# Key projections in three PSUM banks, and GpSimd's weight sums held back by a one-column copy

## The chip, the cores and the metric

The kernel runs on one core of one Trainium2 chip. The metric is the device time of one execution in microseconds (us), in most places as the median of several executions. One profiled execution of each kernel gives a trace with the start and duration of every instruction.

## The reference

A polynomial sketch attention, whose output is the input of four expert layers, mixed by gates:

```python
def phi(x):                                  # x: (4, 4, 1088, 32), S1 and S2: (8, 32)
    a = np.einsum('rd,bhsd->bhsr', S1, x)
    b = np.einsum('rd,bhsd->bhsr', S2, x)
    return np.einsum('bhsi,bhsj->bhsij', a, b).reshape(*x.shape[:-1], 64)
q_p, k_p = phi(q), phi(k)
kv = np.einsum('bhsf,bhsd->bhfd', k_p, v)
num = np.einsum('bhsf,bhfd->bhsd', q_p, kv)
den = np.einsum('bhsf,bhf->bhs', q_p, np.sum(k_p, axis=2))[..., None] + 1e-06
# x = num / den, as (4352, 128)
for e in range(4):                           # F = 1024
    h = np.maximum(x @ w1[e], 0.0)
    out += p[:, e:e + 1] * (h @ w2[e])       # p: gates, scaled to sum 1
```

## The kernel before

The tokens are worked off in chunks. A chunk's expert layers are 16 steps, each a product `h = x w1` into one of three PSUM banks "h", a rectification into `hid` (ScalarE and VectorE) and a product `o = hid w2`. The attention that prepares later tokens is cut into small pieces, laid between the steps. All matmuls go through one helper, which lets two halves of the array (64 columns of weights each) take turns. They run side by side. The trace records each call as two matmuls:

```python
def on_side(out, weights, moving, **flags):
    s = turn[0]
    turn[0] = 1 - s
    nc.tensor.matmul(out(s), weights(s), moving(s), **flags)
```

The keys of batches 1 to 3 pass through this generator. Each `yield` is a place where other work may come between:

```python
def keys(b):
    for r in range(3):
        key_turn(b, r)                          # VectorE transposes
        yield
    for gi in range(3):
        key_project(b, gi, psum(ps_f, "f"))     # 32, 32 and 8 recorded matmuls, then a ScalarE copy to fs
        yield
    ...                                         # products, and key sums in bank "f" again
```

The pool of "f" has one bank, those of "den" and "num" too. A projection into "f" can only start when ScalarE has copied the one before out of it.

The second product of the experts uses sums and differences of blocks of w2. GpSimd forms them, 16 instructions in all; the main loop puts one behind each step from step 13 on:

```python
def weight_sums(e):
    ...
        nc.gpsimd.tensor_tensor(out=out, in0=in0, in1=in1, op=op)    # two inputs in SBUF
        yield
...
        first(i, work)              # h, the rectification, and pieces of attention
        if i > NQ - 4:              # NQ = 16
            next(to_sum, None)
        if i == 2:
            gate_quotients()
        elif i == 5:
            store_gates()           # one VectorE transpose, then transfers
            ...                     # loads of two gates and of the next batch
```

GpSimd has little else to do there, so it runs ahead of the steps: the sums come as soon as it is free, beside VectorE's products for the second unit of 480 queries:

```python
def query_product(qp, p, x, n, qa, qb):
    nc.vector.tensor_tensor(out=qp[p][64*x : 64*x+64, 0:n],
        in0=qa[64*p : 64*p+64, 0:n], in1=qb[64*p : 64*p+64, 0:n], op=ALU.mult)    # two inputs in SBUF
```

These four products are what the matmuls into "den" and "num" wait for.

## Time and profile before

| | before |
|---|---|
| median of the first three executions | 498.6 us (498.53 to 499.03) |
| span of the profiled execution | 496.7 us |
| busy: TensorE matmuls / weight loads / VectorE / ScalarE / GpSimd | 99 / 74 / 65 / 49 / 46% |

A matmul's record includes time in which the next one already runs (a projection's matmul is recorded with 0.22 us, and 32 of them take 1.12 us on the two halves), so a busy TensorE isn't a full one; its waits tell more. In the timeline, a line has the start, the duration, the engine, the source line, the operation, its output and inputs with their shape, and how many instructions it merges; in brackets the idle time ahead of it and what ended that. PE is TensorE's matmuls, PEld its weight loads, DVE VectorE, ACT ScalarE, POOL GpSimd. L188 is the helper's line, so one goes by the names of the tiles: `f<-sk,kT` is a key projection, `fs<-f` its copy, `qp<-qa,qb` the products for the queries, `w2s` the weight sums.

### The profile page before, as it was taken

The page shows a single profiled execution, that of the slowest core. Times are in us where ns is not written, and L with a number is a line of the kernel's source. Part 1 is how long each engine was busy: PE and PEld are TensorE (multiplying, and loading weights), DVE is VectorE, ACT ScalarE, POOL GpSimd, SP SyncE. Part 2 cuts the span into 40 slices and gives each one's busy share as a digit, 9 for nine tenths or more (in the row PEclk, how much of TensorE's full clock was granted, in tenths as well). Part 3 has the DMA queues.
Part 4 walks back from the last instruction along what each step waited for, and adds up shares of the span by engine and source line. Part 5 has one row for each costly group of instructions (what it writes and reads, how often), then busy time and mean ns, then how long its engine had stood idle before and what let it go on. Part 6 is the DMA issues. An engine that isn't in the chain of part 4 may idle for free.

```text
span 496.7 us, 11022 instructions
## 1 busy us (share of the span) xinstructions
PE 489.3 (99%) x4435; PEld 367.8 (74%) x4435; DVE 324.8 (65%) x751; ACT 244.0 (49%) x487; POOL 228.2 (46%) x259
## 2 busy tenths in 40 slices
PE   8999999999999999999999999999999999999996
PEld 6776577777777657777776777777777777778996
DVE  6859756777677485767656747468666656765642
ACT  3334455445444544535455455445455445566651
POOL 6600544444455353434555344334555345655570
PEclk9999999999999999999999999999999999999999
DMA  7881030021002230021002100021001100110000
GB/s 219 270 294 54 0 92 1 2 86 21 0 2 86 66 91 0 1 86 22 1 2 86 21 1 1 2 86 22 2 1 53 23 1 0 45 23 2 15 3 17
DMA packets 29618, 22.36 MB, mean 45 GB/s; under 512 B 19968, under 2 KB 26752, under 8 KB 29184
## 3 DMA queue, kind: packets, MB, share of 16 engines
q1 hardware_dynamic: 29552, 21.66, 15.1%
q8 instruction: 35, 0.57, 0.5%
q14 instruction: 15, 0.12, 0.1%
q10 hardware_dynamic: 16, 0.00, 0.0%
HBM read 19.35 MB, written 2.31 MB: 44 GB/s over the span
## 4 chain that ended last, share of the span: by engine, by line
PE 98%; DVE 1%; issue 0%; ACT 0%; DVEq 0%
PE h L188 49%; PE o L188 40%; PE f L188 5%; PE den L188 2%; PE num L188 1%; PE h L176 1%; DVE qp L412 1%; ACT fs L344 0%; DVE qa L471 0%; DVE end L648 0%; DVE end L644 0%; DVE xT L446 0%; DVE kvz L374 0%; DVE warm L135 0%; DVE s_hl L212 0%
## 5 line engine op out<-in xcount | busy, mean ns | idle before, releaser
L584 DVE SCALAR_TENSOR_TENSOR hid<-h,hid 128x256 f32<-128x256 f32 (+6 forms) x432 | 203.7, 472 | 148.0 <-ACT hid L609 139.7
L188 PE MATMUL h<-xT,w_sb 128*64 128x512 f32 (+4 forms) x1408 | 299.7, 496 | 0.4 <-DVE xT L446 0.4
L609 ACT ACTIVATE hid<-h 128x512 f32<-128x512 f32 (+3 forms) x288 | 158.2, 550 | 200.5 <-PE h L188 169.8
L188 PE MATMUL o<-hid,w2s 128*64 128x256 f32 (+3 forms) x1152 | 220.8, 355 | 0.0
L188 PEld LDWEIGHTS h<-xT,w_sb 128*64 128x64 f32 x1408 | 148.2, 137 | 52.2 <-issue 12.9
L188 PE MATMUL o<-hid,w_sb 128*64 128x256 f32 (+3 forms) x864 | 184.5, 355 | 0.0
L188 PEld LDWEIGHTS o<-hid,w2s 128*64 128x64 f32 x1152 | 133.1, 137 | 29.0 <-issue 2.7
L724 POOL TENSOR_TENSOR ev<-yz,sh 64x256 f32<-64x256 f32 (+3 forms) x72 | 48.5, 674 | 160.5 <-ACT sh L727 154.7
L188 PEld LDWEIGHTS o<-hid,w_sb 128*64 128x64 f32 x864 | 102.4, 137 | 21.4 <-issue 6.6
L712 POOL TENSOR_TENSOR yz<-ev 128x512 f32<-128x512 f32 (+3 forms) x36 | 42.2, 1172 | 80.8 <-ACT ev L715 80.5
L724 POOL TENSOR_TENSOR ct<-ev 128x512 f32<-128x512 f32 (+3 forms) x36 | 42.6, 1182 | 2.8
L724 POOL TENSOR_TENSOR ct<-ct,gate 128x512 f32<-128x512 f32 (+3 forms) x27 | 32.0, 1186 | 2.1
L724 POOL TENSOR_TENSOR total<-total,ct 128x512 f32<-128x512 f32 (+3 forms) x27 | 31.9, 1180 | 2.1
L412 DVE TENSOR_TENSOR qp<-qa,qb 64x352 f32<-64x352 f32 (+2 forms) x44 | 30.2, 687 | 1.1
L714 ACT COPY ev<-o 128x512 f32<-128x512 f32 (+3 forms) x36 | 19.4, 538 | 10.1 <-PE o L188 9.6
L188 PE MATMUL o<-w_sb,hid 128*64 128x128 f32 x256 | 24.2, 273 | 0.0
L188 PEld LDWEIGHTS o<-w_sb,hid 128*64 128x64 f32 x256 | 20.1, 137 | 1.5 <-issue 1.2
L715 ACT COPY ev<-o 128x512 f32<-128x512 f32 (+3 forms) x36 | 19.4, 538 | 2.8 <-PE o L188 0.5
L601 ACT ACTIVATE hid<-h 128x256 f32<-128x256 f32 x24 | 9.2, 383 | 22.8 <-PE h L188 22.3
L351 DVE TENSOR_TENSOR kp<-fs 128x256 f32<-128x256 f32 (+1 forms) x24 | 16.7, 704 | 0.0
L727 ACT COPY sh<-yz 64x256 f32<-64x256 f32 (+3 forms) x36 | 13.7, 379 | 1.6 <-POOL yz L712 0.8
L728 ACT COPY sh<-yz 64x256 f32<-64x256 f32 (+3 forms) x36 | 13.7, 380 | 0.9
(95 smaller groups left out, 244.3 us busy)
## 6 DMA issues: line engine op xcount, KB each, us to landing
w_sb<-in_moe_w_dram SPq DMA_DIRECT2D x8, 512.0 KB, 7.4
gate<-gates SPq DMA_DIRECT2D x3, 1024.0 KB, 4.6
kn<-in_k_dram SPq DMA_DIRECT2D x4, 544.0 KB, 4.0
vn<-in_v_dram SPq DMA_DIRECT2D x16, 128.0 KB, 4.0
gate<-gates SPq DMA_DIRECT2D x2, 960.0 KB
qn<-in_q_dram SPq DMA_DIRECT2D x3, 544.0 KB, 3.8
gate<-gates SPq DMA_DIRECT2D x1, 896.0 KB
out_dram<-ob SPq DMA_DIRECT2D x12, 64.0 KB, 2.0
```

Source lines behind the costliest of these rows:

```text
L188: nc.tensor.matmul(out(s), weights(s), moving(s), **flags)
L351: eng.tensor_tensor(out=_ap(kps[b], 0, P, 256 * t0 + P * p + 64 * x, [[256, n], [32, 2], [R, 4], [1, R]]), in0=_ap(src, 0, P, off + 4 * x, ...
L412: nc.vector.tensor_tensor(out=qp[p][64 * x : 64 * x + 64, 0:n], in0=qa[64 * p : 64 * p + 64, 0:n], in1=qb[64 * p : 64 * p + 64, 0:n], op=A ...
L584: nc.vector.scalar_tensor_tensor(out=out, in0=src, scalar=0.0, in1=in1, op0=ALU.max, op1=ALU.subtract)
L601: nc.scalar.activation(hd[:, 0 : 2 * n], hp[:, 0 : 2 * n], ACTF.Relu)
L609: nc.scalar.activation(hd[:, n * j : n * j + n], hp[:, 0:n], ACTF.Relu)
L712: add = lambda out, in0, in1, op=ALU.add: nc.gpsimd.tensor_tensor(out=out, in0=in0, in1=in1, op=op)
L714: nc.scalar.copy(_ap(ev, 0, P, 0, [[2 * w, 2], [1, w]]), _ap(a0, 0, P, 0, two))
L715: nc.scalar.copy(_ap(ev, 0, P, w, [[2 * w, 2], [1, w]]), _ap(a1, 0, P, 0, two))
L724: add = lambda out, in0, in1, op=ALU.add: nc.gpsimd.tensor_tensor(out=out, in0=in0, in1=in1, op=op)
L727: nc.scalar.copy(sh[HP:P, 0:w], yz[0:HP, 0, 0:w])
L728: nc.scalar.copy(sh[0:HP, 0:w], yz[HP:P, 1, 0:w])
```

## The change

Both parts are meant to take away stops of TensorE: neighbouring projections no longer share a bank, and the sums no longer run beside the products. The second is done with a copy of one column that GpSimd can't make before the second unit's x is there. The sums come behind it in GpSimd's program, and the trace below shows them behind it in time too (27.07 and 27.21 us). The diff in full:

```diff
-        for gi in range(3):
-            key_project(b, gi, psum(ps_f, "f"))
+        for gi, (pool, tag) in enumerate(((ps_f, "f"), (ps_n, "den"), (ps_n, "num"))):
+            key_project(b, gi, psum(pool, tag))
             yield
@@
+    behind = cpool.tile([P, 1], F32, name="behind")
     start()
@@
             first(i, work)
             if i > NQ - 4:
+                if i == NQ - 3:
+
+                    nc.gpsimd.tensor_copy(behind[:, :], xT[:, CHUNKS[0] + CHUNKS[1] - 1 : CHUNKS[0] + CHUNKS[1]])
                 next(to_sum, None)
```

## The prediction

> **What bounds the kernel now.** I read the page from its chain of waits, since an average over the span cannot say where 499 us go. The chain that ended last:
>
> ```profile
> PE 98%; DVE 1%; issue 0%; ACT 0%; DVEq 0%
> PE h L188 49%; PE o L188 40%; PE f L188 5%; PE den L188 2%; PE num L188 1%; PE h L176 1%; DVE qp L412 1%; ACT fs L344 0%; DVE qa L471 0%; DVE end L648 0%; DVE end L644 0%; DVE xT L446 0%; DVE kvz L374 0%; DVE warm L135 0%; DVE s_hl L212 0%
> ```
>
> TensorE carries 98% of the end. 89% is the two products of the expert layers (h and o), which the change doesn't touch. The change can win only time in which TensorE stands still. The next view is the waits by engine, longest first, cut to TensorE's matmuls (PE) and weight loads (PEld); columns are total us, times, longest:
>
> ```profile
> PEld f L188 <- ACT fs L344: 1.7, 3, 0.6
> ...
> PEld den L188 <- DVE qp L412: 1.4, 3, 0.7
> PE f L188 <- ACT fs L344: 0.9, 2, 0.5
> ...
> PE den L188 <- DVE qp L412: 0.4, 1, 0.4
> ```
>
> A PE wait is mostly the same stop as the PEld wait before it, so they must not be added. The two parts of the change aim at exactly these: "f <- fs" is a key projection waiting for ScalarE to copy the one before out of the only bank "f"; "den <- qp" is the attention waiting for VectorE's feature products. Together about 3 us of 499, or 0.6%. That is the ceiling for both parts, and it decides the verdict already. The rest of this text is about how much of it comes back.
>
> The place of the second, in the timeline from 15 to 24 us (start, duration, engine, operation):
>
> ```profile
> 19.75 1.09 DVE L412 TENSOR_TENSOR qp<-qa,qb 64x480 f32<-64x480 f32 x1
> 20.85 1.09 DVE L412 TENSOR_TENSOR qp<-qa,qb 64x480 f32<-64x480 f32 x1
> ...
> 20.29 1.14 POOL L494 TENSOR_TENSOR w2s<-w_sb 128x256 f32<-128x256 f32 x1
> 21.39 1.15 POOL L494 TENSOR_TENSOR w2s<-w_sb,w2s 128x256 f32<-128x256 f32 x1
> ...
> 46.43 0.65 DVE L412 TENSOR_TENSOR qp<-qa,qb 64x480 f32<-64x480 f32 x1
> ...
> 23.79 1.30 PE L188 MATMUL den<-qp,kvz 128*64 128x480 f32 x3 [0.42 <-DVE qp L412]
> 24.48 0.13 PEld L188 LDWEIGHTS den<-qp,kvz 128*64 128x64 f32 x1 [0.50 <-DVE qp L412]
> ```
>
> The same VectorE product takes 1.09 us while GpSimd forms weight sums and 0.65 us (the line at 46.43) when it doesn't; the sums go from 0.73 to 1.14. And the first projections of the second batch:
>
> ```profile
> 61.63 1.01 PEld L188 LDWEIGHTS f<-sk,kT 128*64 128x64 f32 x32 [0.60 <-ACT fs L344]
> 61.64 1.15 PE L188 MATMUL f<-sk,kT 128*64 128x64 f32 x32 [0.46 <-ACT fs L344]
> ```
>
> TensorE stands still while ScalarE's 0.37 us copy empties the bank.
>
> **What the Trainium skill says.** "Perfetto Trace Analysis", Matmuls under Optimizing Tensor Performance, advises that independent matmul groups rotate through different PSUM banks so that one group's evacuation overlaps the next group's matmuls; the 0.46 us gap above is what not rotating costs here. The same page, Identifying the Most-Contended Engine, warns that matmul busy share is no measure of nearness to the limit; agreed, PE shows 99% and the weight loads 74%, so I read stops and not shares. "SBUF — State Buffer", Who interferes with whom, says that a VectorE instruction with two SBUF inputs contends with a GpSimd instruction that reads SBUF, and that one with at most one SBUF input doesn't. The trace agrees in kind: qp (two SBUF inputs) is stretched, while the addition into qf, which reads one input from PSUM, takes 0.66 us with the sums running (17.18) and 0.66 without (38.58). The page says the loser blocks for the whole instruction; 1.09 is less than 0.65 + 0.73, so the measured stretch is what I use.
>
> **Part 1, three banks.** It adds and removes no instruction. The three projections of a batch now go into f, den and num. Batches 1 to 3 use this path (batch 0 has its own), so there are six places where a projection follows another:
> - Batch 1, second projection: the first one's 32 matmuls start at 60.05 and go at about 0.031 us each (1.0 us for 32), so the next could start at 61.07; it starts at 61.64. Won: 0.57. Its third is a step later, without a wait: 0.
> - Batch 2, second: PEld waits 0.48, but four matmuls of h at 0.21 each (from 166.09, one before it) keep the array busy until about 166.73 and the projection starts at 166.84. Won: 0.1.
> - Batch 2, third: could start at 166.84 + 1.0 = 167.85, starts at 168.50. Won: 0.63.
> - Batch 3: expert steps lie between all three, and no wait for fs is shown: 0.
>
> Sum 1.3 us, on the path. Are den and num free? They were last read by VectorE's transpose dT and by the product that writes xT, both ahead of the key transposes on VectorE itself, which the projections need anyway. No new wait there. The attention that next writes den comes many us after the copies.
>
> **Part 2, the held sums.** It adds one GpSimd copy of one column, 0.1 to 0.2 us by the small GpSimd operations at 10 to 12 us (0.12 to 0.30). It depends on the write of xT that ends at 28.19, so the nine sums that ran from 15.92 to 23.22 start after it. On VectorE, three of the four qp products were stretched: 1.09, 1.09 and 0.98 against 0.65, together 0.44 + 0.44 + 0.33 = 1.2 us. The chain from there to den has no other waits, so the last product ends at 24.43 - 1.2 = 23.2 and the one before it at about 22.5. TensorE's loads are free at 23.79 - 0.66 = 23.13. So the first wait (0.66) goes, and of the second (0.50 more) about 0.1 stays. The two 64-column halves of the array run side by side, and both must be through before ScalarE can rectify. A check on that: ScalarE's rectifications come every 0.87 us, but 3.81 us apart (23.47 to 27.28) across den and num. Den and num are four matmul passes of 0.4 us on each half, so 1.6 + 0.87 = 2.47 was due, and 1.3 us were lost. I count **1.15 us** won, all on the path.
>
> What it gives back: the first matmul with a summed weight starts at about 37.1. xT would be ready near 27.0, and sums at 0.73 us each finish expert 0's four by 27.2 + 2.9 = 30.1 and all nine by 33.8, against 36 for that matmul. GpSimd had nothing else from 23.22 to 48.79, so nothing queues behind them. VectorE's work from 27 to 34 (a transpose, hid and end, each with at most one SBUF input or one from PSUM) isn't of the stretched kind.
>
> **Sum.** 1.3 + 1.15 = 2.45 us off 498.6, or 496.15. I take 496.2, because a wait elsewhere may eat a tenth.
>
> **Rivals.**
> 1. Taking away a stop only moves it: the projections finish sooner, and the next h matmul waits for VectorE to free one of the three h banks. For it: PEld h waits for hid 1.3 us in 7 pieces of at most 0.3. Against it: after the projections VectorE had ended its hid at 61.98, before h comes at 63.6. If true for part 1, some 1 us is not won: 497.2.
> 2. The held sums run late, and GpSimd or the first w2s matmul becomes the wait. The slack is some 6 us for expert 0. If xT's hold pushed the sums behind the first collection at 48.8, several us would be lost: 500 or more. The nine sums take 6.6 us in a hole of over 20, so I give this little.
> 3. The waits were never on the path (the other half of the array would have hidden them): 498.6 stays. The 3.81 against 2.47 us speaks against it for part 2, the 98% chain for both.
> 4. More than counted is won, because earlier work upstream also closes small "issue" gaps: 495.3 at best.
>
> **Range and chances.** All rivals but the second lie within 495.3 and 498.6; the three runs before lie within 0.5 us. I set 495.2 to 497.3. Faster by over 2% would need 10 us, three times all of these waits: 0.01. Slower by over 2% needs the second rival at its worst: 0.01. Within 2%: 0.98.
>
> **What would show it.** In the changed kernel: no wait of f, den or num for ScalarE's fs; all four 480-column qp products at 0.65 us; GpSimd's first sum after xT, near 27 us; the wait of den for qp down from 1.4 to 0.3 us or less; the first summed matmul near 36; ratio of busy times unchanged. Wrong would be: sums at 1.1 us again beside other VectorE work, a wait of o for the sums, or a wait of h for hid that grew by as much as was won.

## The result, and the profile after

The changed kernel took 496.11 us (median of 6, 495.90 to 496.64), beside 498.81 us (median of 6, 498.48 to 499.29) for the one before. The ratio is 0.9947 with an interval of 0.9934 to 0.9960, so some 2.6 us are gone.

In the waits view of the changed kernel (total us, times, longest), no wait of f, den or num for fs is left. Of the three waits of den for qp, the short one stays, which belongs to a later unit. GpSimd's new wait is the first line here:

```profile
POOL behind L788 <- DVE xT L446: 11.1, 1, 11.1
...
PEld den L188 <- DVE qp L412: 0.2, 1, 0.2
```

The timeline of the changed kernel from 19 to 37 us, engine by engine:

```profile
19.79 1.31 DVE L412 TENSOR_TENSOR qp<-qa,qb 64x480 f32<-64x480 f32 x2
...
21.90 1.34 DVE L412 TENSOR_TENSOR qp<-qa,qb 64x480 f32<-64x480 f32 x2
...
23.22 1.10 PE L188 MATMUL den<-qp,kvz 128*64 128x480 f32 x4
...
27.07 0.18 POOL L788 COPY behind<-xT 128x1 f32<-128x1 f32 x1 [11.07 <-DVE xT L446]
27.21 0.72 POOL L494 TENSOR_TENSOR w2s<-w_sb 128x256 f32<-128x256 f32 x1
...
32.93 0.73 POOL L494 TENSOR_TENSOR w2s<-w_sb 128x256 f32<-128x256 f32 x1
...
36.27 0.37 PE L188 MATMUL o<-hid,w2s 128*64 128x240 f32 x1
```

The two pairs of products now take 1.31 and 1.34 us where they took 2.19 and 1.67 (19.75 to 21.94, and 22.76 to 24.43). Den starts at 23.22 and not 23.79, and its four matmuls take 1.10 us, where the first three alone took 1.30. The nine sums run from 27.21 to 33.66 and are ready well ahead of the first matmul that uses one, at 36.27.

What the stop cost shows in ScalarE's rectifications, which need both halves of the array. First the pair around den and num in the kernel before, then in the changed one:

```profile
23.47 0.38 ACT L601 ACTIVATE hid<-h 128x256 f32<-128x256 f32 x1 [0.49 <-PE h L188]
27.28 0.38 ACT L601 ACTIVATE hid<-h 128x256 f32<-128x256 f32 x1 [3.42 <-PE h L188]
```

```profile
23.52 0.38 ACT L601 ACTIVATE hid<-h 128x256 f32<-128x256 f32 x1 [0.49 <-PE h L188]
26.09 0.38 ACT L601 ACTIVATE hid<-h 128x256 f32<-128x256 f32 x1 [2.20 <-PE h L188]
```

The pair is 3.81 us apart before and 2.57 after: 1.24 us less.

The second batch's first projections in the changed kernel follow each other without a gap; where the two halves change banks at different moments, the lines alternate:

```profile
58.87 1.19 PE L188 MATMUL f<-sk,kT 128*64 128x64 f32 x29
...
59.90 0.22 PE L188 MATMUL den<-sk,kT 128*64 128x64 f32 x1
59.90 0.22 PE L188 MATMUL f<-sk,kT 128*64 128x64 f32 x1
...
60.28 0.37 ACT L344 COPY fs<-f 128x256 f32<-128x256 f32 x1 [0.36 <-PE f L188]
...
61.21 0.37 ACT L344 COPY fs<-den 128x256 f32<-128x256 f32 x1 [0.56 <-PE den L188]
```

ScalarE empties f while TensorE is already in den.

**A ruler for small differences.** Executions differ by up to 0.7 us in their first 10 us: the first 72 projection matmuls took 2.32 us in the traces of the two kernels above, and 2.41 to 2.80 in eight of the experiments' eleven traces. So I also measure from a fixed event: from the last rectification ahead of den (23.47 before, 23.52 after) to the start of VectorE's last scaling of an output (492.81 before, 490.18 after). That is 469.34 us before and 466.66 after: **2.68 us less**. The copies that collect finished products (36 in each kernel) show where. Counted from the same rectification, they come 0.98 us earlier from the first one (46.4 us), 1.90 earlier by 89 us, 2.68 earlier by 171 us, and then stay there to the end. So everything came from den and from the projections of batches 1 and 2, and nothing was given back later.

### The profile page after: what moved, and what is told of

Same layout as the page of the kernel before. It is cut to its first block, busy times and chain, and to the rows that moved or that the text cites. A ratio compares the mean times of both kernels' runs of the same rounds, so it can differ in the third digit from the quotient of the medians.

```text
span 494.1 us, 11020 instructions
## 1 busy us (share of the span) xinstructions
PE 487.7 (99%) x4435; PEld 373.7 (76%) x4435; DVE 323.2 (65%) x751; ACT 244.2 (49%) x487; POOL 227.2 (46%) x260
## 4 chain that ended last, share of the span: by engine, by line
PE 98%; DVE 1%; DMA 0%; POOL 0%; issue 0%; DVEq 0%
PE h L188 50%; PE o L188 40%; PE f L188 4%; PE den L188 2%; PE num L188 2%; DMA s_raw<-in_S_dram 0%; PE h L176 0%; POOL sr L241 0%; POOL sp L236 0%; DVE end L648 0%; DVE s_e L200 0%; DVE kvz L374 0%; DVE s_f L200 0%; DVE s_T L228 0%; DVE s_hl L227 0%
## 5 line engine op out<-in xcount | busy, mean ns | idle before, releaser
L188 PEld LDWEIGHTS h<-xT,w_sb 128*64 128x64 f32 x1408 | 151.2, 137 | 48.8 <-PE h L176 0.9
L188 PEld LDWEIGHTS o<-hid,w2s 128*64 128x64 f32 x1152 | 131.7, 137 | 29.1
L412 DVE TENSOR_TENSOR qp<-qa,qb 64x352 f32<-64x352 f32 (+2 forms) x44 | 29.1, 661 | 1.1
L188 PE MATMUL o<-w_sb,hid 128*64 128x128 f32 x256 | 22.4, 273 | 0.0
L188 PEld LDWEIGHTS o<-w_sb,hid 128*64 128x64 f32 x256 | 19.0, 137 | 1.5 <-issue 0.2
```

Of the source, the lines that this page charges most:

```text
L412: nc.vector.tensor_tensor(out=qp[p][64 * x : 64 * x + 64, 0:n], in0=qa[64 * p : 64 * p + 64, 0:n], in1=qb[64 * p : 64 * p + 64, 0:n], op=A ...
```

## The experiments

My theory: the two parts act separately, part 1 by having neighbours in different banks (1.46 us), part 2 by keeping GpSimd's SBUF reads away from VectorE's products (1.2 us). Eleven kernels, all correct, five rounds each; they ran in sets on three chips, each set beside the kernel before, whose median was 498.7 to 498.9 us every time. In the table, "ruler" is the length just defined, less that of the kernel before.

| kernel | median us | ratio to before | ruler us |
|---|---|---|---|
| changed kernel | 496.11 | 0.9947 | -2.68 |
| banks_only | 497.38 | 0.9972 | -1.48 |
| hold_only | 498.00 | 0.9984 | -0.98 |
| two_banks | 496.02 | 0.9946 | -2.68 |
| one_bank_num | 498.83 | 1.0001 | 0.00 |
| sums_twice | 497.22 | 0.9970 | -1.54 |
| fills_early | 496.08 | 0.9944 | -2.68 |
| sums_late | 499.70 | 1.0018 | -0.05 |
| hold_gates_later | 497.73 | 0.9981 | -0.98 |
| both_gates_later | 496.48 | 0.9951 | -2.68 |
| hold_free_chain | 497.67 | 0.9977 | -0.98 |
| both_free_chain | 496.51 | 0.9952 | -2.68 |

### banks_only: the first part alone

```diff
# against the changed kernel
-                if i == NQ - 3:
-
-                    nc.gpsimd.tensor_copy(behind[:, :], xT[...])
```

> The three banks without the held sums. My theory: the two parts add up, and in the trace with both, the start of ScalarE's collection copies moved by 0.67 us in the first of the batches with this path and by 0.79 in the second, nothing in the third: 1.46 us in all. So 498.8 - 1.45 = 497.35 us, ratio 0.9971; qp products still at 1.09 us, no wait of f, den or num for fs. Rival (the two parts hide behind each other, so that one alone gives nothing or all): 498.8 or 496.1.

It took 497.38 us, ratio 0.9972 (0.9960 to 0.9985). On the ruler it gains 0.70 us in batch 1 and 0.78 in batch 2. In batch 1 the second projection now starts 0.93 us after the first, where the kernel before needed 1.59 (60.05 to 61.64):

```profile
60.77 1.12 PE L188 MATMUL f<-sk,kT 128*64 128x64 f32 x32
61.70 1.12 PE L188 MATMUL den<-sk,kT 128*64 128x64 f32 x32
```

The wait of den for qp is the old one, no wait for fs is left:

```profile
PEld den L188 <- DVE qp L412: 1.4, 3, 0.7
...
PE den L188 <- DVE qp L412: 0.4, 1, 0.4
```

### hold_only: the second part alone

```diff
# against the changed kernel
-        for gi, (pool, tag) in enumerate(((ps_f, "f"), (ps_n, "den"), (ps_n, "num"))):
-            key_project(b, gi, psum(pool, tag))
+        for gi in range(3):
+            key_project(b, gi, psum(ps_f, "f"))
```

> The held sums with all three projections in bank f. Theory: 1.2 us off, since the rectification after den came 1.19 us earlier with both parts: 497.6 us, ratio 0.9976; waits of f for fs remain at about 1.7 us of weight loads, three times. Rival (parts hide behind each other): 498.8 or 496.1.

It took 498.00 us, ratio 0.9984 (0.9972 to 0.9997): 0.85 us of the median, less than expected and more than nothing. The products are at 0.65 us, and the waits for fs are as they were. Its rectifications around den are 2.58 us apart, so den gave its 1.2 us here too; but the collection copies come only 0.98 us earlier. Where the difference goes shows in the second batch. Its first projection starts at 59.16, which is 35.36 us after the rectification ahead of den, against 36.58 in the kernel before: 1.22 us earlier. The second starts at 60.99, only 0.98 us earlier by the same count:

```profile
59.16 1.37 PE L188 MATMUL f<-sk,kT 128*64 128x64 f32 x32
...
60.99 1.15 PE L188 MATMUL f<-sk,kT 128*64 128x64 f32 x32 [0.46 <-ACT fs L344]
```

The 32 matmuls of the first take 1.37 us from the first start to the last end, where the kernel before needed 1.12: one half of the array is some 0.25 us ahead of the other. The copy must wait for the half behind, and the next projection for the copy, so this lead is not used. With other banks, the half ahead goes on. The parts alone add up to 1.48 + 0.98 = 2.46 us, and together they are 2.68.

### two_banks: are three needed?

```diff
# against the changed kernel
-enumerate(((ps_f, "f"), (ps_n, "den"), (ps_n, "num"))):
+enumerate(((ps_f, "f"), (ps_n, "den"), (ps_f, "f"))):
```

> Held sums, and projections in f, den, f. Theory: what counts is that neighbours are in different banks; by the time of the third projection the copy of the first has ended over 1 us ago. So the same as the changed kernel: 496.1 us, ratio to before 0.9947, and no wait for fs. Rival (three banks are needed): the third projection of the third batch waits as before, some 0.6 us more: 496.7.

It took 496.02 us, ratio 0.9946, the same 2.68 us on the ruler and no wait for fs. Two banks in turn do all of it.

### one_bank_num: is it bank f?

```diff
# against the kernel before
-            key_project(b, gi, psum(ps_f, "f"))
+            key_project(b, gi, psum(ps_n, "num"))
```

> The kernel before, but all three projections in the bank num instead of f: one bank still, another one. Theory: the wait comes from one bank having to be emptied, not from what else uses f (the queries and the key sums), so nothing is won: 498.8 us, ratio 1.000, and the same waits, now of num for fs, 1.7 us of weight loads. Rival (leaving f is what helps, because queries or key sums queue there): part of the 1.45 us is won, 497.4 to 498.

It took 498.83 us, ratio 1.0001 (0.9988 to 1.0013), 0.00 on the ruler. The waits have changed their name and nothing else:

```profile
PEld num L188 <- ACT fs L344: 1.7, 3, 0.6
...
PE num L188 <- ACT fs L344: 0.9, 2, 0.5
```

### sums_twice: GpSimd's reads back beside the products

```diff
# against the changed kernel
                 if i == NQ - 3:
+                    twice = chain.from_iterable(weight_sums(e) for e in range(3))
+                    for _ in range(9):
+                        next(twice)
                     nc.gpsimd.tensor_copy(behind[:, :], xT[...])
```

> The changed kernel, with the nine sums formed twice: once early and unheld, as the kernel before had them, and once behind xT. Theory: the gain of the held sums was the absence of GpSimd's reads beside VectorE's qp products. So those products go back to 1.09, 1.09 and 0.98 us, and den waits again for 1.2 us: 496.1 + 1.2 = 497.3 us. Rival (it was the place of the sums in GpSimd's order, or what they delay later): the held copies still come at 27 us, so 496.1.

It took 497.22 us, ratio 0.9970, so 1.1 us more than the changed kernel; on the ruler 1.14. The held sums are still there, at 28.53 us. The products are slow again:

```profile
19.87 2.21 DVE L412 TENSOR_TENSOR qp<-qa,qb 64x480 f32<-64x480 f32 x2
22.88 1.68 DVE L412 TENSOR_TENSOR qp<-qa,qb 64x480 f32<-64x480 f32 x2
```

So it is what runs beside the products that counts, not what else the sums' new place brings.

### fills_early: GpSimd busy there, but only writing

```diff
# against the changed kernel
                 if i == NQ - 3:
+                    for _ in range(7):
+                        nc.gpsimd.memset(w2s[:, 3, :, :, :], 0.0)      # later overwritten by the sums
                     nc.gpsimd.tensor_copy(behind[:, :], xT[...])
```

> The changed kernel, with seven fills of 128x1024 by GpSimd where the sums used to run, about 1 us each: GpSimd as busy as before, but it reads nothing. Theory: two SBUF inputs of VectorE contend with GpSimd's reads only, so the qp products stay at 0.65 us and the time at 496.1. Rival (any GpSimd work in SBUF slows them): products near 1.1 us, 497.3.

It took 496.08 us, ratio 0.9944, the same 2.68 on the ruler. GpSimd was busy during all but the last 0.28 us of the products, and they didn't get longer:

```profile
16.54 7.02 POOL L788 MEMSET w2s<- 128x1024 f32 x7
...
20.39 1.31 DVE L412 TENSOR_TENSOR qp<-qa,qb 64x480 f32<-64x480 f32 x2
...
22.50 1.34 DVE L412 TENSOR_TENSOR qp<-qa,qb 64x480 f32<-64x480 f32 x2
```

Together with sums_twice this shows that GpSimd's sums, which read SBUF, cost, and fills that only write there don't.

### sums_late: how long could the sums be held?

```diff
# against the changed kernel
                     nc.gpsimd.tensor_copy(behind[:, :], xT[...])
+                    for _ in range(9):
+                        nc.gpsimd.memset(w2s[:, 3, :, :, :], 0.0)
```

> The changed kernel, with nine fills of 128x1024, about 1 us each, between the held copy and the first sum. Tests the slack that I counted: the first four sums would end at 27.2 + 9 + 2.9 = 39.1 us where the first matmul with a summed weight came near 35.9. Theory: TensorE waits 3.2 us there for the sums, all of it on the path: 499.3 us, and the wait is shown as o for w2s. Rival (the slack is longer, or other work fills the wait): 496.1.

The profiled execution took 499.11 us; on the ruler it is 2.63 us longer than the changed kernel. TensorE waits for the third sum, which ends at 38.86 us, and with its weight loads for the fourth, which ends at 39.55:

```profile
36.62 0.57 PE L188 MATMUL o<-hid,w_sb 128*64 128x240 f32 x2
38.92 1.31 PE L188 MATMUL o<-hid,w2s 128*64 128x240 f32 x6 [1.74 <-POOL w2s L494]
...
39.60 0.20 PEld L188 LDWEIGHTS o<-hid,w2s 128*64 128x64 f32 x4 [0.49 <-POOL w2s L494]
```

So the slack was counted about right (2.63 us for 3.2 expected), and held much longer, the sums would eat the gain. The six executions scatter more than any others here: three at 498.54 to 499.19 us with a mean granted clock of 0.999 to 1.000, three at 500.22 to 500.74 with 0.995. Whether the longer stop of TensorE brings on the lower clock is not settled by six executions.

### hold_gates_later and both_gates_later

The 0.22 us that the parts gain together, and one candidate for a better version, led to two pairs of kernels. In the first, the storing of the gates, whose 0.33 us transpose lies between the shuffle and the products on VectorE, comes five steps later:

```diff
# against hold_only, and against the changed kernel
-            elif i == 5:
+            elif i == 10:
                 store_gates()
                 ...            # three loads (two gates, the next batch) move with it
```

> Held sums, one bank, and the storing of the gates (on VectorE one transpose of 0.33 us between the shuffle and the first qp product, then transfers) five steps later, after the last qp product. What it is for: alone, the held sums gave 0.85 us by the clock and 0.98 in the trace, where 1.2 was expected. Theory: the 0.2 us wait that den keeps for its second qp tile leaves one half of the array about 0.25 us ahead of the other, and the next wait for fs, which stops both, takes that lead away. With the transpose gone from the chain the second tile is ready before TensorE asks, neither half leads, and the whole 1.2 us is kept: 497.6 us, collection copies 1.2 us earlier than before when counted from the rectification ahead of den. Rival (the 0.25 us is lost elsewhere): 498.0 and 0.98 us as with the held sums alone.

> The changed kernel with the same move of the gates' storing; the candidate that may beat both. Theory: the last 0.2 us wait of den for qp goes, so 0.2 us less at most: 495.9 us, and no wait of den for qp in the trace. Rival (the lead of one half is worked off by the other anyway): 496.1. A later gate could also delay the first gate products on GpSimd near 55 us, but these have 20 us to arrive.

They took 497.73 us (0.9981) and 496.48 us (0.9951), and stand on the ruler at -0.98 and -2.68, each to 0.01 us where the same kernel stood without the move. The edit failed to do what it was for. In hold_gates_later, VectorE waited for TensorE instead, ahead of a scaling that comes next, so the products ended as late as ever, and den's four matmuls still took 1.10 us. (The 0.2 us wait that the expectation speaks of was misread: in the waits view it is the later unit's. What den itself has left is at most the 0.1 us by which 1.10 exceeds the 1.00 of the next pair.)

```profile
19.54 0.35 DVE L644 TENSOR_SCALAR end<-o,ends 128x128 f32<-128x128 f32 x1 [0.32 <-PE o L188]
```

### hold_free_chain and both_free_chain

So in the second pair that scaling went behind the products too:

```diff
# on top of the edit above; in the last product of the first chunk's first expert
-                    nc.vector.tensor_scalar(out=total[m][:, :], in0=acc[m][:, 0:DM], scalar1=p_e, ...)
+                    later.append(scale)        # the same instruction, given out ahead of the next expert's
```

> Moving the gates' transpose alone freed nothing: VectorE then waited for TensorE in front of the scaling that comes next, and the qp products ended when they had. Here both, the transpose and that scaling (0.33 and 0.35 us), come after the last qp product; held sums, one bank. Theory: the products end some 0.65 us earlier, den waits for nothing, no half of the array leads, and the held sums keep their 1.2 us: collection copies 1.2 us earlier than before counted from the rectification ahead of den, 497.6 us. Rival (the lead of a half isn't what takes 0.25 us): 0.98 us as with the held sums alone, 497.9.

> The same with the three banks; the last candidate. Theory: at most the 0.2 us of den's remaining wait for qp goes: 495.9 us and no such wait in the trace. Rival: 496.1, the wait was hidden by the other half.

They took 497.67 us (0.9977) and 496.51 us (0.9952). This time the edit worked: the last product ends 0.81 us ahead of the rectification in hold_free_chain (23.21 and 24.02), and 0.27 in hold_only (23.53 and 23.80). Den's matmuls start in step, 1.00 us for the four instead of 1.10, and the rectifications around den are 2.48 us apart instead of 2.58. Yet the ruler shows -0.98 and -2.68 again. So the 0.1 us won at den is gone by the end, and my theory that den's remaining wait gives one half its lead falls: with den in step, hold_free_chain's first projection is again spread out:

```profile
57.67 0.57 PE L188 MATMUL h<-xT,w_sb 128*64 128x480 f32 x1
...
58.04 1.77 PE L188 MATMUL h<-xT,w_sb 128*64 128x480 f32 x7
59.28 1.46 PE L188 MATMUL f<-sk,kT 128*64 128x64 f32 x32
```

The source and the traces point to where the lead comes from, though no run tested it. In these chunks a step's second product is seven calls that take turns, so one half gets four and the other three, and the next step does the reverse. A call lasts some 0.4 us here (two matmuls, 0.2 us apart), so the halves are in step and 0.4 us apart by turns. In hold_free_chain they leave den and num in step (0.04 us), and the step ahead of the first projection finds them 0.37 us apart (57.67 and 58.04 above). In the kernel before, the stop at den leaves one half 0.43 us ahead (its next h begins at 26.15, the other's at 26.58), which swaps the turns: there the step ahead of the projection finds them in step (eight matmuls of h in 1.80 us from 58.44), and the projection takes 1.12 us. That the lead is thrown away at the wait for fs, and kept with other banks, is what the traces show. Neither candidate beats the changed kernel. Their medians are 0.4 us above it, but with the same length on the ruler and a start that is 0.6 us later in their profiled executions. Traces of one_bank_num and fills_early, whose edits act only after that start, have it too (rectification at 24.19 and 24.11); whether the two edits here have a part in it isn't settled.

## Why the prediction was right

- **The total.** Predicted 496.2 us, measured 496.11; predicted 2.45 us off, measured 2.7 by the medians and 2.68 on the ruler.
- **The bound and the ceiling.** TensorE stayed 98% of the chain of waits. Only its stops could be won, and their sum (3 us) bounded the gain.
- **Part 1, 1.3 us: right, a little small.** Alone it gave 1.47 us by the medians and 1.48 on the ruler. Batch 1: 0.57 predicted, 0.70 measured. The prediction let a projection last 1.02 us before the next; it lasts 0.93 (60.77 to 61.70 in banks_only), which is 0.09 of the difference. The rest is the second projection, 0.98 us to the next matmul after the wait and 0.94 without it. Batch 2: two terms were off and largely cancelled. The second projection gained nothing where 0.1 was predicted (1.79 us behind the first in both kernels, 165.05 to 166.84 and 165.06 to 166.85), so that its wait was hidden by h altogether; the third gained 0.78, not 0.63. Batch 3: 0 and 0.
- **No new wait in den or num: right.** No run with these banks shows one; two_banks shows that num wasn't needed.
- **Part 2, 1.15 us: right on top of part 1, too large alone.** On top of the three banks it gave 1.20 on the ruler (2.68 - 1.48). Alone it gave 0.98 there and 0.85 by the medians. The text treated the parts as independent, and the term that it lacked is the 0.22 us which a wait in bank f takes back from it. That its 1.15 us hit the sum so well needed the other part beside it.
- **The mechanism of part 2: right, and shown** by sums_twice (reads: slow, 1.14 us lost) and fills_early (writes: nothing lost).
- **What it gives back: right.** All sums ended at 33.66 (predicted 33.8), and the first matmul that uses one came at 36.27. (In the kernel before that matmul starts at 37.45; the 37.1 of the prediction is the one ahead of it, with a plain weight.) Rival 2 came about only when sums_late held the sums 9 us longer, and then cost 2.63 us.
- **The other rivals.** A stop that only moves (rival 1) would have left h waiting for hid; the waits view of the changed kernel shows no such wait. That the waits were off the path (rival 3) is refuted by the 1.48 us of part 1. Of rival 4, 0.2 us more than counted came true, but not for its reason: the terms above were too small by 0.18 (part 1) and 0.05 us (part 2). Most of the "issue" gaps closed in hold_only (weight loads of h: 13.5 to 1.9 us), which won less than counted.
- **A sign that I misnamed.** "Ratio of busy times unchanged" was loose: the weight loads' busy time rose from 367.8 to 373.7 us for the same 4435 loads. Their single times add up to the same in both traces (607.6 and 607.5 us), so they overlap each other less; no run tested why.

## What to carry to other kernels

When one engine is on the path for 98% of the span, add up its waits by cause before judging a change: the sum is the ceiling, and here it said "under 1%" at once. Let neighbouring groups of matmuls alternate between two banks if an engine must empty one between them; more than two won nothing here. Before moving work to an idle GpSimd, look at what VectorE does then: reads from SBUF beside a VectorE operation with two SBUF inputs cost (here 1.09 us and not 0.65 for a product), and a copy that depends on the right tile is a cheap way (0.18 us) to hold such work back, as long as its user has slack.

## What the Trainium skill lacked or had wrong

- "SBUF — State Buffer", Summary: rules for kernel authors: it says that of VectorE and GpSimd the second to come blocks fully until the first has finished. Here VectorE's products rose from 0.65 to 1.09 us and GpSimd's sums from 0.73 to 1.14 while both ran, starting in turn every 0.54 to 0.56 us (19.75, 20.29, 20.85, 21.39). That fits blocking by turns, if about half of each record is waiting: the product that starts at 22.76, behind a sum that ends at 23.22, ends at 23.74. No run shows the waiting itself. What the page lacks is the cost: one pair took 1.1 us, and 0.65 + 0.73 would be 1.38, so whole records aren't what excludes the other. What the page says under Who interferes with whom of a GpSimd instruction that only writes is right: beside fills, the products stayed at 0.64 to 0.66.
- "TensorE: Matmul & The Clock Gate", The mechanism: it says that matmuls are strictly in order, in start and in end. Between the two 64-column halves they aren't in this trace, where the calls for den all stand ahead of num's in the kernel's source. In the kernel before, a matmul of num on one half starts ahead of the last one of den on the other, and its (modelled) end is earlier too:

```profile
24.65 0.57 PE L188 MATMUL num<-qp,kvz 128*64 128x480 f32 x1
24.93 0.57 PE L188 MATMUL den<-qp,kvz 128*64 128x480 f32 x1
```

- No page that I found says what this lead of one half is worth: here 0.22 us of a 1.2 us gain were lost at a wait that stops both halves.
- "Perfetto Trace Analysis", Matmuls: the advice to rotate through banks holds. The section doesn't say how many banks neighbouring groups need; with the held sums, two banks in turn gave all of the 2.68 us that three gave.
